# Seven block products instead of eight in the out-projection of the last four units of an RWKV + MLP kernel

## The chip, the cores and the metric

One core of one Trainium2 chip runs the kernel. The metric is the device time of one execution in microseconds (us), the median of several runs. TensorE (PE in the profile) multiplies matrices, VectorE (DVE), ScalarE (ACT) and GpSimd (POOL) work elementwise, SyncE (SP) issues most of the transfers. "PEld" is the loading of a matmul's stationary operand, which the profile shows as an instruction of its own.

## The reference

An RWKV-6 attention block feeds a two-layer MLP. Everything is float32.

```python
# attention: B, H, S, D = 4, 8, 768, 48
for t in range(S):
    cur = einsum('bhd,bhe->bhde', u[None] * k[:, :, t], v[:, :, t])
    y[:, :, t] = einsum('bhd,bhde->bhe', r[:, :, t], state + cur)
    state = w[:, :, t][:, :, :, None] * state + einsum('bhd,bhe->bhde', k[:, :, t], v[:, :, t])
x = y.transpose(0, 2, 1, 3).reshape(3072, 384)
# MLP: d_model = 384, d_ff = 2048
h = x @ w_in                       # (3072, 384) @ (384, 2048)
g = h * erf(softplus(h))
out = g @ w_out                    # (3072, 2048) @ (2048, 384)
```

## The kernel before

**Units and steps.** The 3072 tokens are cut into 12 units of 256 tokens: two batches (`NJ = 2`, index `j`) times 128 positions (`C`). Step `s` of the main loop does the attention of unit `s`. The MLP follows at a distance: `hidden(s - 1)` computes and activates the hidden values of the unit before, and `project(s - 3)` is the out-projection of the unit three back. In `in_order(s, k)` a letter string says how the pieces are laid between the parts of a step: `P` is one piece of `project`, `H` one piece of `hidden`, `A` one call of `advance`, which runs waiting activation stages (softplus or erf on ACT, or the DVE product `h * erf(...)`) from the list `later`. Steps up to 4 use `attend`, later ones `attend_late`. After step 11, the last, the loop `for k in range(1, 15)` runs what is left: the rest of `project(9)`, `hidden(11)`, `project(10)`, `project(11)`.

**Order.** The whole program stands in a manual schedule: each engine takes its instructions in the order in which the code issues them, and waits by semaphore for its operands and for buffers to come free. So an instruction that waits holds up what stands behind it on its own engine.

**The MLP's tiles.** `hidden` keeps the activated values of a unit in two tiles (`gs[0]`, `gs[1]`), one for each half of d_ff; each is 128 partitions (d_ff within a block) x 8 blocks (`FG`) x 256 tokens. `w_in_sb` and `w_out_sb` hold the weights for the whole kernel. `hidden` (L742) does three matmuls of 128x128 by 128x256 for each of the 16 blocks, and ACT copies each pair out of PSUM (L751). `project` (L771) does for each batch `j` 16 matmuls with a 128x128 stationary block of `gs` and 384 moving columns of `w_out_sb`, accumulates them in one PSUM tile (`ps_m`, two buffers, shared with `hidden`), copies that with ACT (L780) and sends it out on the SP queue (L781). Eight pieces (`P`) of four matmuls make one unit. Each float32 matmul stands in the profile as two pieces: 12 units x 32 matmuls are the "x768" of L771, 12 x 48 the "x1152" of L742.

**The activations.** For each of the two tiles ACT runs softplus (L724) and erf (L727), each behind a load of its function table, and DVE multiplies in two halves of 128x1024 (L731).

**Attention in the late steps.** `attend_late(s)` begins with PE products of the unit before (`from_own`, L478), a DVE `fence` (L487) that PE's next products wait for, level products (L444), and `through_state` (L504), which ends the unit before; its result goes by ACT and DMA into `xT`, which `hidden` reads. Alongside, `prepare(s + 1)` readies the next unit with POOL products (L312, L374, L378), DVE products and sums, and a last part: `scale` at the near level (L260), then the product of `block_sb` with `by_tokens` (L418), which comes back from DRAM.

**Buffers named below.** `rk1` (pool `att`) is scratch of the attention; `w` (pool `ins`) holds an input; `words` (pool `wide`, three buffers) holds inputs by rows and scratch. The last of them are read in the preparation of unit 11, which takes place in step 10.

Of the kernel before, what the change touches and what calls it, by code (L numbers as in the profile page):

```python
# [11 lines left out]
FP32 = mybir.dt.float32  # L12
I32 = mybir.dt.int32
# [2 lines left out]
ALU = mybir.AluOpType  # L16

P = 128
EP = 64
HC = 64  # L20
NC = 2
NJ = 2
FG = 8
# [37 lines left out]
def kernel(  # L61
# [14 lines left out]
    nc = tc.nc  # L76
    PSUM = bass.MemoryType.PSUM

    n_steps, _, _, JP, C = rkw.shape
# [4 lines left out]
    _, NT, DM = w_out.shape  # L84
    KT = DM // P
    UNIT = NJ * C
    NG = NT // FG
    SPC = NB // NJ
# [3 lines left out]
    const = ctx.enter_context(tc.tile_pool(name="const", bufs=1))  # L92
    ins = ctx.enter_context(tc.tile_pool(name="ins", bufs=2))
    att = ctx.enter_context(tc.tile_pool(name="att", bufs=2))
    xs = ctx.enter_context(tc.tile_pool(name="xs", bufs=3))
    hid = ctx.enter_context(tc.tile_pool(name="hid", bufs=4))
    act = ctx.enter_context(tc.tile_pool(name="act", bufs=2))
    wide = ctx.enter_context(tc.tile_pool(name="wide", bufs=4))
    outs = ctx.enter_context(tc.tile_pool(name="outs", bufs=2))
# [3 lines left out]
    ps_m = ctx.enter_context(tc.tile_pool(name="ps_m", bufs=2, space=PSUM))  # L103
# [17 lines left out]
    u_row = const.tile([P, D], FP32, name="u_row")  # L121
    w_in_sb = const.tile([P, NT, DM], FP32, name="w_in_sb")
    w_out_sb = const.tile([P, NT, DM], FP32, name="w_out_sb")
    y = ps_y.tile([P, NE, NJ, NP // 2, C], FP32, name="y")

    turns = {"next": 0, "converting": False}
# [40 lines left out]
    def near_log(s):  # L167
        return NEAR_LOG - (s == DIRECT)
# [85 lines left out]
    def scale(s, level):  # L254

        in_t, tots = loaded[s][0], ready[s][1]
        half, nb = 1 << (level - 1), JP * C >> level
        n = 1 if s > DIRECT and level == LOG else 2
        halves = view(in_t[:, 0:2], half, [[JP * C - half, n], [2 * half, nb], [1, half]])
        nc.vector.tensor_mul(  # L260
            halves, halves, view(tots[level - 1], 0, [[1, n], [2, nb], [0, half]])
        )

    def prepare(s):
# [3 lines left out]
        if s < DIRECT:  # L268
            rk1 = att.tile([P, 2, JP, C], FP32, name="rk1", bufs=1)
# [59 lines left out]
        else:  # L329
# [4 lines left out]
            to = over_blocks[:].rearrange("p (h b) n -> p b h n", h=NC)  # L334
# [76 lines left out]
        if near == NEAR:  # L411
# [2 lines left out]
                out=kTs[s][:], in_=k_blocks[:].rearrange("(g b) s d -> (b s) g d", g=NH)  # L414
            )
        scale(s, near_log(s))
        nb = HC // NEAR
        nc.vector.tensor_mul(  # L418
            own[:].rearrange("p n (b t) -> p n b t", t=NEAR),
# [2 lines left out]
            ),  # L422
            by_tokens[:, :, None, :].to_broadcast([P, NH, nb, NEAR]),
        )

    kTs, spread = {}, {}

# [136 lines left out]
    def attend_late(s, place):  # L564

        c, in_t, vt, own, S, S_next, ends = parts_of(s)
        RK = in_t[:, 0:2]
        before = s - 1 if s - 1 > DIRECT else None
        if before:
            from_own(before, ready[before][0], 1)  # L570
            fence()
        pp = products([P, NE, JP, HC])
        level_products(pp, RK, LOG - 1)
        scale(s, LOG - 1)
        take_level(own, pp, LOG - 1)
        if before:
            from_own(before, ready[before][0], 0)
            through_state(before, xTs[before])
            if s + 1 < n_steps:
                load_step(s + 1)  # L580
        following = prepare(s + 1) if s + 1 < n_steps else iter(())
        next(following, None)
        nc.gpsimd.tensor_mul(faded[0][:], S[:], ends[:, :, 0:1].to_broadcast([P, JP, D]))
        next(following, None)
        kT = kTs[s]
        nc.vector.tensor_mul(
            kT[:].rearrange("p (e n) d -> p n e d", e=NE),
            kT[:].rearrange("p (e n) d -> p n e d", e=NE), spread[s][:],
        )
        place(0)  # L590
        next(following, None)
        place(1)

        pp = products([P, NE, JP, HC])
        level_products(pp, RK, LOG)
        if s + 1 < n_steps:
            spread_blocks(s + 1, pp)
        take_level(own, pp, LOG)
        ps = products([P, NC, JP, HC])
        ps = [ps[:, h] for h in range(NC)]  # L600
        state_part(s, kT, ps)
        scale(s, LOG)
        for e in range(NE):
            nc.vector.tensor_add(middle[rows(e)], faded[0][rows(e)], ps[0][rows(e), :, :D])
        place(2)
        next(following, None)
        if s < n_steps - SPC:
            nc.gpsimd.tensor_mul(
                faded[1][:], middle[:], ends[:, :, 1:2].to_broadcast([P, JP, D])
            )  # L610
            for e in range(NE):
                nc.vector.tensor_add(S_next[rows(e)], faded[1][rows(e)], ps[1][rows(e), :, :D])
        place(3)
        for _ in following:
            pass
        place(4)
# [95 lines left out]

    later = []

    def hidden(xT, gs, cut):


        def activate(h):

            held = []  # L720

            def softplus():
                held.append(act.tile([P, FG, UNIT], FP32, name="sp"))
                nc.scalar.activation(held[0][:], h[:], AF.Softplus)  # L724

            def erf():
                nc.scalar.activation(held[0][:], held[0][:], AF.Erf)  # L727

            def multiply():
                for part in (slice(0, FG // 2), slice(FG // 2, FG)):  # L730
                    nc.vector.tensor_mul(h[:, part], h[:, part], held[0][:, part])  # L731

            later.extend([(softplus, True), (erf, True), (multiply, False)])

        for g in range(NG):
            h = hid.tile([P, FG, UNIT], FP32, name="h")
            gs.append(h)
            for f in range(0, FG, FT):
                ps = ps_m.tile([P, FT, UNIT], FP32, name="m")
                for ff in range(FT):  # L740
                    for kk in range(KT):
                        nc.tensor.matmul(  # L742
                            ps[:, ff, :],
                            lhsT=w_in_sb[:, g * FG + f + ff, kk * P : (kk + 1) * P],
                            rhs=xT[:, kk, :],
                            start=kk == 0,
                            stop=kk == KT - 1,
                        )
                    if cut and not ff and g == NG - 1 and f == FG - FT:
                        yield  # L750
                nc.scalar.copy(h[:, f : f + FT, :], ps[:])  # L751
                if f == FG - FT:
                    activate(h)
                yield

    def project(s, gs):

        c, i = divmod(s, SPC)
        ps = [None] * NJ

        halves = [slice(0, FG // 2), slice(FG // 2, FG)]
        for g in range(NG):
            for j, part in (
                [(j, part) for part in halves for j in range(NJ)]
                if not s and g == NG - 1
                else [(j, part) for j in range(NJ) for part in halves]
            ):
                if not g and not part.start:
                    ps[j] = ps_m.tile([P, DM], FP32, name="m")
                for f in range(FG)[part]:  # L770
                    nc.tensor.matmul(  # L771
                        ps[j][:],
                        lhsT=gs[g][:, f, j * C : (j + 1) * C],
                        rhs=w_out_sb[:, g * FG + f, :],
                        start=g + f == 0,
                        stop=g == NG - 1 and f == FG - 1,
                    )
                    if g == NG - 1 and f == FG - 1:
                        o = outs.tile([P, DM], FP32, name="o")
                        nc.scalar.copy(o[:], ps[j][:])  # L780
                        nc.sync.dma_start(out=out[i * NJ + j, c], in_=o[:])  # L781
                    if f % 4 == 3:
                        yield

    xTs, hids, projs = {}, {}, {}
    gated = [[] for _ in range(n_steps)]

# [18 lines left out]
    def piece(kind, of):  # L806
        if not 0 <= of < n_steps:
            return
        if of not in kind:
            kind[of] = hidden(xTs[of], gated[of], not of) if kind is hids else project(of, gated[of])  # L810
        next(kind[of])

    def in_order(s, k):


        order = ("APPPAPP", "APPP", "HH", "AHHH", "AHHH", "PPAPP")
        if s == DIRECT:
            order = ("APPP", "APPP", "APPHH", "AHHH", "AHHH")
        for what in order[k]:
            if what == "A":  # L820
                advance()
            elif what == "P":
                piece(projs, s - 3)
            else:
                piece(hids, s - 1)
# [13 lines left out]
    }  # L839
    ALONE = {1, 2}  # L840

    make_identity(nc, ident[:])
    nc.vector.memset(y[:], 0.0)
    nc.vector.memset(sums[:], 0.0)
# [176 lines left out]
```

## Time and profile before

| | |
|---|---|
| median of 3 runs | 616.99 us (616.94 to 617.49) |
| span of the profiled execution | 614.9 us |
| PE busy | 602.1 us (98%), 6858 matmul pieces |
| DVE busy | 409.3 us (67%) |
| ACT busy | 293.9 us (48%) |
| POOL busy | 293.3 us (48%) |
| L771 (out-projection) | 252.1 us busy, 768 pieces |
| L742 (hidden) | 257.3 us busy, 1152 pieces |

The span runs from the first to the last instruction or transfer that the profile shows; the device time that is compared between kernels holds in addition what lies around it. No separate device time is given for the profiled execution; the median of the runs is 2.1 us above the span. "Busy" is the union of the records of an engine. The mean duration of a record is its latency: matmuls overlap, so the time from one to the next is read from the busy time of a stretch divided by its pieces.

### The profile page before, as it was taken

The page shows a single profiled execution, that of the slowest core. Times are in us where ns is not written, and L with a number is a line of the kernel's source. Part 1 is how long each engine was busy: PE and PEld are TensorE (multiplying, and loading weights), DVE is VectorE, ACT ScalarE, POOL GpSimd, SP SyncE. Part 2 cuts the span into 40 slices and gives each one's busy share as a digit, 9 for nine tenths or more (in the row PEclk, how much of TensorE's full clock was granted, in tenths as well). Part 3 has the DMA queues.
Part 4 walks back from the last instruction along what each step waited for, and adds up shares of the span by engine and source line. Part 5 has one row for each costly group of instructions (what it writes and reads, how often), then busy time and mean ns, then how long its engine had stood idle before and what let it go on. Part 6 is the DMA issues. An engine that isn't in the chain of part 4 may idle for free.

```text
span 614.9 us, 15592 instructions
## 1 busy us (share of the span) xinstructions
PE 602.1 (98%) x6858; PEld 445.9 (73%) x6858; DVE 409.3 (67%) x459; ACT 293.9 (48%) x374; POOL 293.3 (48%) x295
## 2 busy tenths in 40 slices
PE   7889999999999999999999999999999999999997
PEld 6668787678668668668668768768768768668654
DVE  5687696995995897897797797797797311110300
ACT  2548888544446724534534534534534444624600
POOL 4348184603497399299199299299296000000000
PEclk9999999999999999999999999999999999999999
DMA  8376471440353316307307306405303100000000
GB/s 325 117 281 203 184 258 58 164 149 8 136 157 78 101 34 190 112 29 206 101 30 197 109 31 181 126 31 156 117 28 79 25 26 0 9 26 1 0 27 26
DMA packets 51371, 63.27 MB, mean 103 GB/s; under 512 B 34920, under 2 KB 40296, under 8 KB 49896
## 3 DMA queue, kind: packets, MB, share of 16 engines
q1 hardware_dynamic: 50152, 61.68, 31.5%
q8 instruction: 54, 0.88, 0.6%
q10 hardware_dynamic: 1152, 0.59, 0.4%
q14 instruction: 13, 0.11, 0.1%
HBM read 52.39 MB, written 8.69 MB: 99 GB/s over the span
## 4 chain that ended last, share of the span: by engine, by line
PE 85%; DVE 6%; DMA 3%; POOL 2%; issue 2%; ACT 1%; SPq 0%; POOLq 0%; ACTq 0%; DVEq 0%
PE m L771 38%; PE m L742 37%; PE pp L444 4%; DMA w<-in_rkw 3%; PE y L478 2%; PE y L504 1%; PE pp L530 1%; DVE in L260 1%; POOL w_in_sb L229 1%; DVE w_in_sb L225 1%; POOL tot_sb L312 1%; PE pp L673 1%; DVE sums L364 1%; DVE pp L217 1%; DVE own L456 1%
## 5 line engine op out<-in xcount | busy, mean ns | idle before, releaser
L742 PE MATMUL m<-xT,w_in_sb 128*128 128x256 f32 x1152 | 257.3, 382 | 2.4 <-DVE w_in_sb L225 1.2
L771 PE MATMUL m<-w_out_sb,h 128*128 128x384 f32 x768 | 252.1, 488 | 0.0
L742 PEld LDWEIGHTS m<-xT,w_in_sb 128*128 128x128 f32 x1152 | 216.1, 190 | 34.8 <-issue 3.6
L771 PEld LDWEIGHTS m<-w_out_sb,h 128*128 128x128 f32 x768 | 144.6, 190 | 98.5
L751 ACT COPY h<-m 128x512 f32<-128x512 f32 x96 | 56.1, 584 | 130.5 <-PE m L742 130.4
L731 DVE TENSOR_TENSOR h<-h,sp 128x1024 f32<-128x1024 f32 x48 | 74.6, 1594 | 52.1 <-ACT sp L727 51.9
L260 DVE TENSOR_TENSOR in<-in,tot_sb 128x1024 f32<-128x1024 f32 (+1 forms) x60 | 84.4, 1414 | 30.6 <-PE pp L444 27.3
L378 POOL TENSOR_TENSOR words<-words,rest 128x528 f32<-128x528 f32 (+10 forms) x77 | 85.7, 1113 | 6.0
L374 POOL TENSOR_TENSOR rk<-words 128x528 f32<-128x528 f32 (+3 forms) x28 | 44.5, 1588 | 81.2 <-DVE sums L364 70.8
L780 ACT COPY o<-m 128x384 f32<-128x384 f32 x24 | 11.5, 480 | 110.3 <-PE m L771 110.3
L312 POOL TENSOR_TENSOR tot_sb<-tot_sb 128x256 f32<-128x256 f32 (+4 forms) x60 | 54.6, 911 | 4.5
L727 ACT ACTIVATE sp<-sp 128x2048 f32<-128x2048 f32 x24 | 45.9, 1911 | 0.3
L724 ACT ACTIVATE sp<-h 128x2048 f32<-128x2048 f32 x24 | 45.9, 1911 | 0.3
L444 PEld LDWEIGHTS pp<-in 48*64 48x64 f32 (+1 forms) x2368 | 33.8, 125 | 16.3 <-issue 8.5
L364 DVE TENSOR_REDUCE sums<-words 128x6 f32<-128x288 f32 (+8 forms) x66 | 29.2, 470 | 19.4 <-POOL words L374 19.2
L444 PE MATMUL pp<-in 48*64 48x64 f32 (+1 forms) x2368 | 38.3, 212 | 3.7 <-issue 1.6
L727 ACT ACT_TABLE_LOAD x24 | 30.8, 1283 | 15.9 <-issue 13.0
L374 POOL TENSOR_TENSOR words<-words 128x336 f32<-128x336 f32 (+6 forms) x49 | 35.1, 716 | 3.8
L364 DVE TENSOR_REDUCE sums<-rk 128x14 f32<-128x672 f32 (+9 forms) x54 | 34.8, 704 | 0.2
L724 ACT ACT_TABLE_LOAD x24 | 30.8, 1283 | 4.9 <-issue 4.5
L378 DVE TENSOR_TENSOR words<-words,rest 128x576 f32<-128x576 f32 (+8 forms) x34 | 27.9, 820 | 1.2
L229 POOL TENSOR_TENSOR w_out_sb<-w_out_sb,rest 128x768 int32<-128x768 int32 x8 | 17.8, 2222 | 17.8 <-DVE w_out_sb L225 17.7
(80 smaller groups left out, 438.0 us busy)
## 6 DMA issues: line engine op xcount, KB each, us to landing
in<-in_rkw SPq DMA_DIRECT2D x11, 1024.0 KB, 5.6
words<-in_moe_w_in SPq DMA_DIRECT2D x8, 768.0 KB, 4.5
words<-in_moe_w_out SPq DMA_DIRECT2D x8, 768.0 KB, 4.3
words<-in_rk_rows SPq DMA_DIRECT2D x8, 768.0 KB, 6.8
w<-in_rkw SPq DMA_DIRECT2D x11, 512.0 KB, 8.4
v<-in_v SPq DMA_DIRECT2D x12, 384.0 KB, 6.9
out<-o SPq DMA_DIRECT2D x24, 192.0 KB, 1.9
rest<-in_w_rows SPq DMA_DIRECT2D x8, 384.0 KB, 7.3
```

What stands on the lines that cost most here:

```text
L260: nc.vector.tensor_mul(halves, halves, view(tots[level - 1], 0, [[1, n], [2, nb], [0, half]]))
L312: nc.gpsimd.tensor_mul(new, pair[:, :, 0], pair[:, :, 1])
L364: nc.vector.tensor_reduce(out=view(sums[:], n, [[near * (NEAR + 1), NEAR // near], [NEAR + 1, near - n]]), in_=terms[n], axis=mybir.AxisLi ...
L374: engine.tensor_mul(terms[n], r[:, :, n:], k[:, :, : near - n])
L378: engine.tensor_mul(k[:, :, :m], k[:, :, :m], w[:, :, n : n + m])
L444: nc.tensor.matmul(pp[s0 : s0 + m, e, n, :m], lhsT=rk[rows(e), 1, n, s0 : s0 + m], rhs=rk[rows(e), 0, n, t0 : t0 + m], start=True, stop=True,)
L724: nc.scalar.activation(held[0][:], h[:], AF.Softplus)
L727: nc.scalar.activation(held[0][:], held[0][:], AF.Erf)
L731: nc.vector.tensor_mul(h[:, part], h[:, part], held[0][:, part])
L742: nc.tensor.matmul(ps[:, ff, :], lhsT=w_in_sb[:, g * FG + f + ff, kk * P : (kk + 1) * P], rhs=xT[:, kk, :], start=kk == 0, stop=kk == KT - 1,)
L751: nc.scalar.copy(h[:, f : f + FT, :], ps[:])
L771: nc.tensor.matmul(ps[j][:], lhsT=gs[g][:, f, j * C : (j + 1) * C], rhs=w_out_sb[:, g * FG + f, :], start=g + f == 0, stop=g == NG - 1 and ...
```

## The change

The products of the last four units (`FAST = 8`: units 8 to 11) take another form. For a unit, the activations are a 2 x 2 block matrix (batch `j` by half of d_ff) and so are the weights (half of d_ff by half of the 384 output columns, 192 each). Instead of the eight block products of the plain form, `project_fast` does seven (the Strassen-Winograd form), each of eight matmuls 128x128 by 128x192. It needs:

- sums of the weights, made by `mix_weights` in four DVE operations of 128x1536 elements: three go into the new tile `mixed`, the fourth replaces a quarter of `w_out_sb` in place. They are issued in the last part of `prepare(9)`, `prepare(10)` and `prepare(11)`, that is, in steps 8, 9 and 10; in step 10 there are two.
- sums of the activations, made by `blend` in four DVE operations of 128x1024 for each unit. For unit 8 they are issued in step 11, ahead of the `kT` product; for units 9 to 11 they follow the last activation product of the unit in `later`.
- recombination: ACT copies of PSUM after the first, third and fourth product, and a DVE addition after the sixth and after the seventh, behind each of which an output row block is sent out.

The seven products are seven pieces; from step 11 on the letter strings have seven `P` for a unit instead of eight. The pool `xs` (the tiles `xT`) has two buffers instead of three, and the DMA scratch is set to 1024; the sums of activations use `rk1`, `w` and `words`.

```diff
+FAST = 8
-    xs = ctx.enter_context(tc.tile_pool(name="xs", bufs=3))
+    xs = ctx.enter_context(tc.tile_pool(name="xs", bufs=2))
+    ND = DM // NJ
+    mixed = const.tile([P, 3, FG, ND], FP32, name="mixed")
...
         scale(s, near_log(s))
+        if s > FAST:
+            next(mixing)
         nb = HC // NEAR
         nc.vector.tensor_mul(
             own[:].rearrange("p n (b t) -> p n b t", t=NEAR),
...
+        if s == FAST + 3:
+            next(mixing)
...
         next(following, None)
+        if s == FAST + 3:
+            blend(FAST, gated[FAST])
         kT = kTs[s]
...
             later.extend([(softplus, True), (erf, True), (multiply, False)])
+            if of > FAST and len(gs) == NG:
+                later.append((lambda: blend(of, gs), False))
...
+    def mix_weights():
+        upper, lower = w_out_sb[:, :FG], w_out_sb[:, FG:]
+        b11, b12, b21, b22 = (x[:, :, k * ND : (k + 1) * ND] for x in (upper, lower) for k in range(2))
+        t3, t2, t4 = (mixed[:, n] for n in range(3))
+        nc.vector.tensor_sub(t3, b22, b12)
+        yield
+        nc.vector.tensor_add(t2, t3, b11)
+        yield
+        nc.vector.tensor_sub(t4, b21, t2)
+        yield
+        nc.vector.tensor_sub(b12, b12, b11)
+        yield
...
+    def blend(of, gs):
...
+        nc.vector.tensor_add(s1, a21, a22)
+        nc.vector.tensor_sub(s2, s1, a11)
+        nc.vector.tensor_sub(s4, a12, s2)
+        nc.vector.tensor_sub(a21, a11, a21)
+        blends[of] = s1, s2, a21, s4
...
+    def project_fast(s, gs):
...
+        product(m0[:, lo], a11, b11, True)
+        nc.scalar.copy(o[0][:, lo], m0[:, lo])
+        yield
+        product(m1[:, lo], a22, t4, True)
+        yield
+        product(m1[:, hi], s1, t1, False)
+        nc.scalar.copy(o[1][:], m1[:])
+        yield
+        product(m0[:, lo], s2, t2, False)
+        nc.scalar.copy(o[0][:, hi], m0[:, lo])
+        yield
+        product(m1[:, hi], s4, b22, False)
+        yield
+        product(m0[:, lo], s3, t3, False)
+        halves = o[1][:].rearrange("p (k n) -> p k n", k=2)
+        nc.vector.tensor_add(halves, halves, m0[:, None, lo].to_broadcast([P, 2, ND]))
+        nc.sync.dma_start(out=out[i * NJ + 1, c], in_=o[1][:])
+        yield
+        product(m1[:, lo], a12, b21, True)
+        nc.vector.tensor_add(o[0][:], o[0][:], m1[:])
+        nc.sync.dma_start(out=out[i * NJ, c], in_=o[0][:])
+        yield
...
-            kind[of] = hidden(xTs[of], gated[of], not of) if kind is hids else project(of, gated[of])
+            if kind is hids:
+                kind[of] = hidden(of, xTs[of], gated[of], not of)
+            else:
+                kind[of] = (project_fast if of >= FAST else project)(of, gated[of])
...
         order = ("APPPAPP", "APPP", "HH", "AHHH", "AHHH", "PPAPP")
+        if s >= FAST + 3:
+            order = ("PAPPPAP", "PAP", "HH", "AHHH", "AHHH", "PPPAP")
...
+    mixing = mix_weights()
-    nc = bacc.Bacc("TRN2", target_bir_lowering=False, num_devices=1)
+    nc = bacc.Bacc("TRN2", target_bir_lowering=False, num_devices=1, dynamic_dma_scratch_size=1024)
```

## The prediction

> **What bounds the kernel now.** I read the page first: busy shares, slices, chain. Then the chain in order of time, for the last fifth of the run.
>
> ```profile
> span 614.9 us, 15592 instructions
> PE 602.1 (98%) x6858; PEld 445.9 (73%) x6858; DVE 409.3 (67%) x459; ACT 293.9 (48%) x374; POOL 293.3 (48%) x295
> ...
> PE   7889999999999999999999999999999999999997
> PEld 6668787678668668668668768768768768668654
> DVE  5687696995995897897797797797797311110300
> ...
> PEclk9999999999999999999999999999999999999999
> ```
>
> PE is busy all the time from the fourth slice on, at the full granted clock. DVE has gaps of two to three tenths in steps 5 to 10 and is nearly idle from slice 32 on (step 11 and the tail).
>
> ```profile
> 531.24 18.26 PE m L771 x56
> 549.49 20.72 PE m L742 x96
> 570.21 41.29 PE m L771 x128
> 611.57 0.48 ACT o L780
> ```
>
> The chain at the end is nothing but MLP matmuls one behind another. So PE time taken out of units 8 to 11 comes off the end one for one, as long as nothing new makes PE wait. Two questions remain: what a piece with 192 columns costs, and whether DVE delivers its sums in time.
>
> **The price of a piece.** I take it from stretches where PE does only one kind: 64 pieces of 384 columns in 20.84 us (436.81 to 457.65) are 0.3256 us each, and 96 pieces of 256 columns in 20.92 us (366.45 to 387.37, in the chain) are 0.2179 us. The line through both has 0.000841 us a column and about 2.5 ns fixed, so 192 columns cost 0.2179 - 64 x 0.000841 = 0.164 us. Before, four units took 256 x 0.3256 = 83.4 us. Now they take 4 units x 7 products x 8 matmuls x 2 pieces = 448 pieces x 0.164 = 73.5 us. **The sum for PE: 9.9 us less**, 2.46 us a unit.
>
> That holds only if the loads of the stationary operand, 448 instead of 256, stay hidden:
>
> ```profile
> 436.81:457.65 20.84, 20.84 (x64) 12.01 (x64) 1.00 0.24 85
> ```
> ```profile
> L771 PEld LDWEIGHTS m<-w_out_sb,h 128*128 128x128 f32 x768 | 144.6, 190 | 98.5
> ```
> ```profile
> L852 PEld LDWEIGHTS m<-ident 128*128 128x128 f32 x19 | 2.2, 192 | 0.0
> ```
> ```profile
> 183.80 0.86 PEld L673 LDWEIGHTS pp<-ident,in 128*128 128x128 f32 x8
> 183.80 1.09 PE L673 MATMUL pp<-ident,in 128*128 128x128 f32 x8
> ```
>
> The first line is the projection of one unit (columns: stretch, length, PE busy, loads busy): 64 loads fill 12.01 us, 0.188 us each, so nowhere in L771 do two loads overlap each other. A record of 0.190 us is longer than the 0.164 us that I want to give a piece; if 0.190 were the rate, there would be no gain. The third line decides: in the warm-up from 6 to 8 us, 19 loads of 0.192 us stand in 2.2 us, so they overlap and come every 0.116 us or faster, each with a 128-column matmul behind it. The transposes of L673, with a different stationary block each time, load 8 in 0.86 us, 0.108 us each. 0.190 is a latency, and 0.116 is under 0.164.
>
> [...] the L771 pieces follow each other at 0.3256 us, what 384 columns cost at the slope alone (0.323), so there is no room for a load in series. I use the row.
>
> For the 192-column piece the ends are 0.160 us (slope alone: 71.7 us, 11.7 us less) and 0.190 us (85.1 us, 1.8 us more); I take 0.164, because the slope joins measured rows and the warm-up shows loads faster than that. Some products wait for two engines, for which PE may need a separate semaphore instruction; the five in L771 last 0.051 us. If all 28 products paid one, that would be 1.4 us; I take 0, since the L771 stretches show no such gap, and keep it in the range.
>
> **DVE: sums of weights.** No row has 128x1536. With POOL idle, 128x768 takes 0.947 us (L586 in step 11) and 128x1024 takes 1.222 us (L731 after 480 us), so 1536 cost about 1.77 us. At the place where they go in steps 8 and 9, the scale just ahead takes 1.42 us instead of 1.21 with POOL running, so 2.07 us there; with the worst factor on the page's shape (2.1 against 1.21) 3.1. The cover is DVE's wait:
>
> ```profile
> 384.67 1.23 DVE L418 TENSOR_TENSOR own<-block_sb,by_tokens 128x1024 f32<-128x1024 f32 x1 [0.34 <-DMA by_tokens<-by_blocks]
> 388.03 0.17 DVE L487 COPY seen<-y 128x16 f32<-128x16 f32 x1 [2.13 <-PE y L478]
> ...
> 434.31 0.17 DVE L487 COPY seen<-y 128x16 f32<-128x16 f32 x1 [2.46 <-PE y L478]
> ...
> 476.79 1.23 DVE L418 TENSOR_TENSOR own<-block_sb,by_tokens 128x1024 f32<-128x1024 f32 x1 [2.02 <-DMA by_tokens<-by_blocks]
> 480.87 0.17 DVE L487 COPY seen<-y 128x16 f32<-128x16 f32 x1 [2.86 <-PE y L478]
> ```
>
> The fence L487 is what PE's second group of L478 waits for, and behind the new operation only L418 and the fence stand in its way. Step 8: 0.34 + 2.13 = 2.47 us idle against 2.07. Step 9: 2.46 against 2.07. Step 10: 2.02 + 2.86 = 4.88 against 2 x 1.77 = 3.54; the in-place one waits for project(7), which PE has done in the first half of the step. PE itself needs the fence only about 0.5 us later (388.66). Cost taken: 0; at 3.1 us each, about 0.1 us in each of two steps.
>
> **DVE: unit 8 in step 11.** Four sums at 1.22 us start where kT started, 483.56, and end at 488.5. PE begins product 1 at 483.08 and one product lasts 16 x 0.164 = 2.63 us. Product 3 (s1) begins at 488.3 and s1 is there at 484.8; product 4 at 491.0 needs s2 (486.0) and the ACT copy of product 1, which stands behind ACT's DMA issues until 486.94 and is done at 487.4. The kT product ends at 489.5; the activation product behind it started at 490.18 before anyway. Cost 0.
>
> **DVE and ACT: units 9 and 10.** Their blends run after 506 and 545 in a DVE that was idle for 18 and 31 us there; they are needed more than 12 us later. Cost 0.
>
> **Unit 11** is the tight one. Project(10) now begins at 570.21 - 2 x 2.46 = 565.3 and ends at 583.7. ACT has copies of 0.3 to 0.5 us and three activation stages of 1.28 + 1.91 = 3.19 us between them: copy 1 at 568.3, erf 571.5, copy 576.1, softplus 579.3, erf 582.5. DVE is worse: the addition behind product 7 waits for PE until 583.7 and ends at 584.3 (0.55 us, as L604), and behind it on DVE stand the last activation product (2 x 1.22, to 586.7), then s1 (587.9), s2 (589.2), s4, s3 (591.6). PE: product 1 of unit 11 needs only the first tile, 583.7 to 586.3; product 2 needs the second tile's first half at 586.3 (there at 585.5) and its second at 587.6 (586.7); product 3 needs s1 at 588.9, 1.0 us after it is there; the others have over 2 us. Cost 0, with a reserve of 0.8 to 1.0 us.
>
> **Rest.** The last ACT copy (0.48) becomes a DVE addition (about 0.55): +0.07 us. The output transfers are as many and as large; the two of a unit change order, and SP has nothing else to do there but xT's. With two `xT` buffers, a write waits for hidden() of two units back, which PE ended a step earlier: 0. The DMA scratch: every queue on the page is "hardware_dynamic" or "instruction" and none is named for such a scratch, so 0.
>
> **Sum.** 614.9 - 9.86 + 0.07 = 605.1 us span. The median of the runs lies 2.1 us above the span of the profiled execution, which I keep: **607.2 us**.
>
> **Rivals.** (a) DVE late at unit 11 or at a fence. If sums and activation products took 1.77 us there, as L260 does beside POOL, s1 would come at 589.6, 0.6 us late; with the fences (0.2) and the semaphore instructions (1.4) about 2 us: 609.4. POOL is idle after slice 32, which speaks against it. (b) Load-bound pieces, the slower side: PE cannot overlap loads when each has a fresh operand[...]. At 0.190 us a piece the change costs 85.1 - 83.4 = +1.8 us: 618.8. It decides from 83.4 / 448 = 0.186 us on. The L771 loads that never overlap speak for it, L852 and L673 against. (c) Half of that: loads at about 0.175 us, 78.4 us, 612. (d) The change does not do what it says: the sevenths are not saved because products repeat; the instruction order has 56 matmuls of 192 columns a unit in place of 32 of 384, so no.
>
> **Chances.** Forecast as worked out 0.80 (606 to 608.4), (a) 0.11, (b) 0.05, (c) 0.03, anything else 0.01. The range 606.0 to 609.7 takes in the forecast and (a). About 0.2%, 1.2 us, is what a measurement of this kernel can tell from no change: faster 0.93, same 0.02, slower 0.05.
>
> **What would show it.** Right: the new product line has 448 pieces in about 73.5 us; a unit's seven products take 18.4 us; loads of that line overlap each other; PE waits for DVE nowhere at its third product; hidden(11) begins at about 544.6 and the last product ends at 601.7. Wrong: 0.19 us a piece with PEld full (b); a PE wait on a `blend` result, or fence waits gone in steps 8 and 9 with PE idle before L478's second group (a).

## The result, and the profile after

The changed kernel takes 608.01 us (median of 4 runs, 607.56 to 609.0) against 617.24 us for the kernel before (the three executions of the table above and a fourth): 0.9851 of its time, 95% interval 0.9837 to 0.9865. A second series gave 607.39 us against 617.23 us: 0.9837 (0.9823 to 0.9850). The forecast was 607.2 us, with a range of 606.0 to 609.7. Some executions of these kernels have a mean granted clock of 0.992 to 0.997 and are 1 to 4 us longer than the others of the same kernel; all eight of the changed kernel here have 0.999 or 1.00.

The page of the changed kernel: its head and some of its slices:

```profile
span 605.9 us, 16024 instructions
...
PE 592.9 (98%) x7050; PEld 470.8 (78%) x7050; DVE 439.5 (73%) x487; ACT 294.3 (49%) x378; POOL 296.1 (49%) x295
...
PE   8889999999999999999999999999999999999997
...
PEclk9999999999999999999999999999999999999999
```

PE is as full as before and at the same clock, over a span that is 9.0 us shorter, with 192 matmul pieces more. DVE has 30 us more work (409.3 to 439.5). The line numbers move: `project` is L782 now, and the new products are L844, `hidden` is L753, the fence is L494.

The end of the chain of waits, in order of time (start, length, what):

```profile
483.72 18.40 PE m L844 x112
...
525.17 2.80 PE m L844 x16
...
529.46 15.80 PE m L844 x96
545.25 20.72 PE m L753 x96
565.97 36.41 PE m L844 x224
602.47 0.56 DVE o L868
```

The reader sees the same chain as before: MLP matmuls one behind another, with no link to DVE between them. Units 10 and 11 take 36.41 us where they took 41.29.

### The profile page after: what moved, and what is told of

It reads as the page before. It is cut to its first block, busy times and chain, and to the rows that moved or that the text cites. A ratio compares the mean times of both kernels' runs of the same rounds, so it can differ in the third digit from the quotient of the medians.

```text
span 605.9 us, 16024 instructions
## 1 busy us (share of the span) xinstructions
PE 592.9 (98%) x7050; PEld 470.8 (78%) x7050; DVE 439.5 (73%) x487; ACT 294.3 (49%) x378; POOL 296.1 (49%) x295
## 4 chain that ended last, share of the span: by engine, by line
PE 85%; DVE 7%; issue 2%; POOL 2%; ACT 2%; DMA 1%; SPq 0%; DVEq 0%; POOLq 0%; ACTq 0%
PE m L753 38%; PE m L782 25%; PE m L844 12%; PE pp L451 5%; DVE in L263 2%; PE y L485 2%; PE y L511 1%; PE pp L537 1%; POOL w_in_sb L232 1%; DMA in<-in_rkw 1%; DVE w_in_sb L228 1%; PE pp L682 1%; DVE sums L367 1%; DVE pp L220 1%; DVE own L463 1%
## 5 line engine op out<-in xcount | busy, mean ns | idle before, releaser
L753 PE MATMUL m<-xT,w_in_sb 128*128 128x256 f32 x1152 | 257.3, 382 | 2.4 <-DVE w_in_sb L228 1.2
L753 PEld LDWEIGHTS m<-xT,w_in_sb 128*128 128x128 f32 x1152 | 216.1, 190 | 34.6 <-issue 3.6
L782 PE MATMUL m<-w_out_sb,h 128*128 128x384 f32 x512 | 168.6, 489 | 0.0
L782 PEld LDWEIGHTS m<-w_out_sb,h 128*128 128x128 f32 x512 | 96.2, 190 | 65.3
L315 POOL TENSOR_TENSOR tot_sb<-tot_sb 128x256 f32<-128x256 f32 (+4 forms) x60 | 57.6, 960 | 4.5
L451 PEld LDWEIGHTS pp<-in 48*64 48x64 f32 (+1 forms) x2368 | 33.8, 125 | 16.1 <-issue 8.3
L451 PE MATMUL pp<-in 48*64 48x64 f32 (+1 forms) x2368 | 38.4, 212 | 3.8 <-issue 1.6
L791 ACT COPY o<-m 128x384 f32<-128x384 f32 x16 | 7.7, 478 | 65.6 <-PE m L782 65.6
```

The source lines that it names most:

```text
L315: nc.gpsimd.tensor_mul(new, pair[:, :, 0], pair[:, :, 1])
L451: nc.tensor.matmul(pp[s0 : s0 + m, e, n, :m], lhsT=rk[rows(e), 1, n, s0 : s0 + m], rhs=rk[rows(e), 0, n, t0 : t0 + m], start=True, stop=True,)
L753: nc.tensor.matmul(ps[:, ff, :], lhsT=w_in_sb[:, g * FG + f + ff, kk * P : (kk + 1) * P], rhs=xT[:, kk, :], start=kk == 0, stop=kk == KT - 1,)
L782: nc.tensor.matmul(ps[j][:], lhsT=gs[g][:, f, j * C : (j + 1) * C], rhs=w_out_sb[:, g * FG + f, :], start=g + f == 0, stop=g == NG - 1 and ...
```

## The experiments

**1. What a load costs: fewer columns.** Everything rests on the price of a piece. Cutting the same products into narrower pieces makes the loads more and the columns of each fewer, until the load shows.

```diff
+        parts = {8: 2, 9: 3, 10: 4, 11: 1}[s]
         def product(to, a, b, start):
-            for f in range(FG):
-                nc.tensor.matmul(to, lhsT=a[:, f], rhs=b[:, f], ...
+            n = ND // parts
+            for q in range(parts):
+                part = slice(q * n, (q + 1) * n)
+                for f in range(FG):
+                    nc.tensor.matmul(to[:, part], lhsT=a[:, f], rhs=b[:, f, part], ...
```

> The seven products of units 8, 9 and 10 are cut into columns: two pieces of 96, three of 64, four of 48 in place of one of 192, each with all its stationary blocks loaded again; unit 11 stays at 192. The arithmetic is the same. Theory (a piece costs its columns as long as that is more than the time of a load): the changed kernel has 0.1625 us for 192 columns; if loads never bind, 96, 64 and 48 columns cost 0.082, 0.056 and 0.042 us and the three units stay at 18.4 to 19 us each, under 2 us in all. If a load of 128 columns takes about 0.107 us and hides behind the matmul before it, all three kinds cost about 0.107 us: the units take 24.0, 36.0 and 47.9 us, some 53 us more than the changed kernel. Rival (a load holds the engine 0.190 us, or cannot overlap with a matmul): 0.19 us a piece, 42.6, 63.8 and 85.1 us, over 135 us more.

It took 707.8 us. PE's timeline shows two later products of each kind, and then two of unit 11 at 192 columns (start, length, instructions):

```profile
486.94 3.74 PE L849 MATMUL m<-mixed,h 128*128 128x96 f32 x32
490.51 3.74 PE L849 MATMUL m<-w_out_sb,rk 128*128 128x96 f32 x32
...
543.92 5.52 PE L849 MATMUL m<-w_out_sb,words 128*128 128x64 f32 x48
549.28 5.52 PE L849 MATMUL m<-mixed,words 128*128 128x64 f32 x48
...
613.00 13.85 PE L849 MATMUL m<-w_out_sb,rk 128*128 128x48 f32 x64
626.65 13.85 PE L849 MATMUL m<-mixed,rk 128*128 128x48 f32 x64
...
689.09 2.76 PE L849 MATMUL m<-w_out_sb,words 128*128 128x192 f32 x16
691.69 2.76 PE L849 MATMUL m<-mixed,words 128*128 128x192 f32 x16
```

The record of one piece is longer than the time to the next (0.326 us at 192 columns in the changed kernel), so the price is read from start to start: (490.51 - 486.94) / 32 = 0.1116 us at 96 columns, (549.28 - 543.92) / 48 = 0.1117 us at 64, 2.60 / 16 = 0.1625 us at 192. Two widths with one price: the columns no longer set it. It is not the mere issue of instructions either: the 64 short attention products of L451, each with its own smaller load, take 0.93 us in the chain of the changed kernel, 0.0145 us each. What is left is the load: 241 loads stand in the 26.80 us of the later 64-column products, and PE is busy all that time. So a load of 128x128 comes every 0.112 us (the expectation took 0.107; the eight loads of L673 in 0.86 us, which the prediction shows, are 0.108 us each), hidden behind running matmuls, and by an estimate it binds below about 131 columns (0.112 us on the line through 0.1625 us at 192 and 41.29 / 128 = 0.3226 us at 384). The change at 192 columns lies on the safe side, by a factor of 1.45 in time. Rival (b), 0.190 us a piece, falls.

Units 8 and 9 took 25.2 and 37.7 us, where 24.0 and 36.0 were expected. Unit 10 took 89.8 us instead of 47.9: the 48-column pieces shown cost 13.65 / 64 = 0.213 us, twice as much, which neither theory expected. The next run is about that.

**2. The clock at 48 columns.** The edit is the same with `{8: 4, 9: 1, 10: 3, 11: 4}`.

> As the run cut into columns, with another assignment: unit 8 and unit 11 in pieces of 48 columns, unit 10 in pieces of 64, unit 9 at 192. There the 48-column unit ran at half the granted clock from its first product on, and the 64-column unit at the full one. [...]units 8 and 11 both drop to 0.213 us a piece (95 us a unit) and unit 10 stays at 0.112; if it was the length of the MLP stretch without attention, or its place at the end of the run, unit 8 keeps the full clock at 0.112 us a piece (50 us).

774.58 us. First unit 8's first product, then a table by stretch for the later products of unit 8 (48 columns), unit 10 (64) and unit 11 (48); the columns of the table are the stretch, its length, PE busy, loads busy, granted clock, DMA:

```profile
483.18 8.72 PE L849 MATMUL m<-w_out_sb,h 128*128 128x48 f32 x64
```

```profile
491.71:573.62 81.91, 81.91 (x385) 81.91 (x385) 0.50 0.01 3
646.11:672.91 26.80, 26.80 (x243) 26.80 (x242) 1.00 0.00 1
687.19:755.45 68.26, 68.26 (x321) 68.26 (x322) 0.50 0.00 1
```

Wherever the 48 columns stand, PE counts as busy all the time, and yet the granted clock is 0.50 in these stretches. It does not start so, as the expectation had it: unit 8's first product takes only 8.53 us from start to start. The clock is 1.00 for its first 5.7 us, in which pieces of 48 columns follow each other every 0.112 us like those of 64 and 96, and then falls to 0.50; unit 11 here and unit 10 of run 1 show the same after 5.2 and 6.2 us. So the load has one price at three widths, and the step to 0.213 us comes with the clock: at 0.50 the loads too come every 0.213 us (385 in 81.91 us). At 64 columns the clock stays at 1.00 for 27 us. So position and the absence of attention are ruled out. The fall goes with the width, 48 columns against 64; what in the width brings it about is not shown.

**3. The sums alone.** The sums are made at their places, into scratch, and the out-projection stays plain.

```diff
-        nc.vector.tensor_sub(b12, b12, b11)
+        nc.vector.tensor_sub(t3, b12, b11)
-        nc.vector.tensor_sub(a21, a11, a21)
+        nc.vector.tensor_sub(s1, a11, a21)
-                kind[of] = (project_fast if of >= FAST else project)(of, gated[of])
+                kind[of] = project(of, gated[of])
-        if s >= FAST + 3:
-            order = ("PAPPPAP", "PAP", "HH", "AHHH", "AHHH", "PPPAP")
```

> All sums of weights and activations are made at the same places as in the changed kernel, but into scratch, and the out-projection stays in its plain form with 384 columns for all units; the sums are read by nobody. Theory (DVE's waits cover the sums): no difference to the kernel before beyond 0.3 us, 616.9 to 617.5; fence waits of about 0.8 us left in steps 8 and 9. Rival (sums or the new layout of buffers cost PE time): 0.6 us or more above the kernel before, with idle PE at the fence of steps 8 to 10 or at the start of the kernel.

617.59 us against 617.29: 1.0009 (1.0000 to 1.0018), 0.1 us above the expected range and at the edge of what can be told from nothing. Single executions go from 616.6 to 619.9 us here and from 616.6 to 619.1 in the kernel before. Without those at a mean granted clock of 0.994 to 0.997, five of 20 here and three of 23 there, the medians are 617.45 and 617.26 us. The first trace has a span of 616.3 us and still shows fence waits of 0.77 and 0.73 us in steps 8 and 9. A second trace was taken of the same kernel:

> The kernel with all sums made and the plain out-projection kept, once more for its trace; its timed runs went from 616.6 to 619.9 us. Theory: the sums cost PE nothing, and what differs from the kernel before lies in PE's stalls without a releaser (1.55 us in step 6 in its first trace, 0.94 us in the kernel before). Rival: PE waits for the fence or for sums.

617.49 us. In this trace step 8's out-projection begins at 344.32 us, in the first at 344.90, in the kernel before at 343.96; from there to the beginning of the last stretch of matmuls (570.73, 571.31 and 570.21) all three need 226.3 to 226.4 us, and that stretch takes 41.29 us in each. The sums cost PE at most 0.2 us; the rest of the difference between these traces lies ahead of step 8, where no sum is made yet.

**4. The products alone.**

```diff
-        if s > FAST:
-            next(mixing)
-        if s == FAST + 3:
-            next(mixing)
-        if s == FAST + 3:
-            blend(FAST, gated[FAST])
-            if of > FAST and len(gs) == NG:
-                later.append((lambda: blend(of, gs), False))
-        s1, s2, s3, s4 = blends[s]
+        a21 = gs[0][:, :, C:]
+        s1, s2, s3, s4 = a21, a12, a21, a22
-        t3, t2, t4 = (mixed[:, n] for n in range(3))
+        t3, t2, t4 = b22, b21, t1
```

> The seven products without any sums: the sums of weights and of activations are left out and each product takes a plain block of the activations and of the weights, so the output is not the reference's; copies, additions and transfers stay. Theory (the sums are fully covered): the same as the changed kernel within 0.5 us, 607.4 to 608.5, seven products in 18.2 to 18.4 us. Rival (products of units 8 to 11 wait for sums): 1 us or more faster than the changed kernel, below 607.

607.54 us, 0.984 of the kernel before (0.9823 to 0.9856). From the first product of unit 8 to the beginning of the last addition its chain has 483.45 to 602.19, 118.74 us; the changed kernel has 483.72 to 602.47, 118.75 us. With all sums taken away, PE gains nothing there: they are fully covered.

**5. The reserve at unit 11.**

```diff
-        nc.vector.tensor_add(s1, a21, a22)
+        for _ in range(3 if of == 11 else 1):
+            nc.vector.tensor_add(s1, a21, a22)
```

> The first activation sum of unit 11 alone is issued three times instead of once (the same result). In the changed kernel it ended at 588.34 us and the third product of unit 11, which reads it, began at 589.21: a reserve of 0.87 us. Theory: two more at 1.26 us put its end at 590.86, product 3 begins 1.65 us late, and everything behind it follows: 1.65 us slower than the changed kernel, about 609.7. Rival (the wait is absorbed, because weight loads and later products can go ahead, or because the end is set by the outputs): under 0.3 us slower.

609.5 us (0.9887, 0.9844 to 0.9931), 1.5 us above the first series of the changed kernel and 2.1 above the second. Its four executions go from 608.55 to 613.58 us, the last at a mean granted clock of 0.992. The trace shows the wait where it was forecast. First DVE and PE of the changed kernel, then PE of this one:

```profile
584.26 0.55 DVE L868 TENSOR_TENSOR o<-o,m 128x384 f32<-128x384 f32 x1 [2.04 <-PE m L844]
584.74 2.35 DVE L740 TENSOR_TENSOR h<-h,sp 128x1024 f32<-128x1024 f32 x2
587.12 1.22 DVE L823 TENSOR_TENSOR words<-h 128x1024 f32<-128x1024 f32 x1
```

```profile
589.21 2.76 PE L844 MATMUL m<-w_out_sb,words 128*128 128x192 f32 x16
```

```profile
591.13 2.87 PE L845 MATMUL m<-w_out_sb,words 128*128 128x192 f32 x16 [1.55 <-DVE words L824]
```

In the changed kernel s1 is there at 588.34 and product 3 begins at 589.21, 0.87 us later. Two repeats of 1.26 us eat that and leave 1.65; PE waits 1.55 us for `words`, and all that follows moves with it. So the addition behind product 7, for which DVE waits while the last activation product stands behind it, is the place with the smallest reserve of the change.

**6. The reserve at the fence.** The weight sums of steps 8 and 9 twice:

```diff
-        nc.vector.tensor_sub(t3, b22, b12)
+        for _ in range(2):
+            nc.vector.tensor_sub(t3, b22, b12)
-        nc.vector.tensor_add(t2, t3, b11)
+        for _ in range(2):
+            nc.vector.tensor_add(t2, t3, b11)
```

> The weight sums of steps 8 and 9 are each issued twice (the same result): 1.84 us more on DVE ahead of the fence in each of the two steps. In the changed kernel the fence still waited 0.76 us for PE there, and PE's next group of products reads the fence's mark about 0.5 us after it. Theory (that wait is all the cover there is): the fence comes 1.08 us later in both steps and PE stands still for 0.5 to 0.6 us in each, some 1.1 us slower than the changed kernel. Rival (DVE's lateness passes on to the next step, where other waits take it up, and PE does not see it): under 0.3 us slower. Second rival (it adds up through the chain of DVE, GpSimd and fence): 2 us or more.

610.7 us in the median of 608.61, 610.1, 611.29 and 611.78; the trace is of the first. Two more traces were taken of the same kernel:

> The kernel with the weight sums of steps 8 and 9 issued twice, once more for its trace: its timed runs spread from 608.6 to 611.8 us while the traced one was 608.6, with 0.6 and 0.4 us more in front of PE's second group in steps 8 and 9. If the spread comes from the chain of DVE, GpSimd and fence, a slower execution shows longer fence waits of PE in steps 8 to 10 (over 1.5 us in all); if it comes from PE's stalls without a releaser, those in steps 6 and 10 are longer (over 2 us in all) and the fence waits are as before.

> The same a third time: a slower execution shows either longer fence waits of PE in steps 8 to 10, or longer PE stalls without a releaser in steps 6 and 10.

608.75 and 609.07 us. All three traces agree on the wait. Step 8 in the changed kernel, DVE and PE, then in the first trace of this run, DVE and PE:

```profile
384.65 1.84 DVE L801 TENSOR_TENSOR mixed<-w_out_sb 128x1536 f32<-128x1536 f32 x1
...
388.43 0.17 DVE L494 COPY seen<-y 128x16 f32<-128x16 f32 x1 [0.76 <-PE y L485]
```

```profile
387.70 0.66 PE L485 MATMUL y<-own,v 64*48 64x64 f32 x32
389.12 0.63 PE L485 MATMUL y<-own,v 64*48 64x64 f32 x32
```

```profile
388.65 1.23 DVE L423 TENSOR_TENSOR own<-block_sb,by_tokens 128x1024 f32<-128x1024 f32 x1
389.92 0.17 DVE L494 COPY seen<-y 128x16 f32<-128x16 f32 x1
```

```profile
388.14 0.67 PE L485 MATMUL y<-own,v 64*48 64x64 f32 x32
390.15 0.66 PE L485 MATMUL y<-own,v 64*48 64x64 f32 x32 [0.41 <-DVE seen L494]
```

From the first to the second group of L485 it is 2.01 us here (388.14 to 390.15) and 1.42 us in the changed kernel (387.70 to 389.12): 0.59 us more, and 0.38 us more in step 9. In step 8 the other two traces have 2.03 and 1.99 us. The sum, 1.0 us, is the difference of the spans (606.8 against 605.8 us in the second series' trace). The theory holds for what the traces show.

The median is another matter: it lies 3.3 us above the changed kernel, which is the second rival's figure, but that rival's chain is in no trace. The three executions above 610 us have mean granted clocks of 0.997, 0.997 and 0.992, the first has 1.00. The third trace, at 0.997, shows what such a mean can be: one spell of about 3.4 us at half the clock, between 15 and 22 us, after which step 5's out-projection begins at 205.19 instead of 204.33 us. Neither its fence waits nor its stop in step 6 (1.02 us, 1.36 in the first trace) is longer. No trace holds an execution above 610 us, so when their clock falls, and how much of their time that takes, stays open.

**7. A fifth unit.** If PE alone sets the end, unit 7 should give another 2.4 us. Its sums do not fit into DVE's step 10, so GpSimd makes them, in the hole in its work:

```diff
-        if s > FAST:
+        if FAST - 1 <= s <= FAST + 2:
             next(mixing)
...
+        if s == FAST + 2:
+            blend_early(FAST - 1)
...
+    def blend_early(of):
...
+        nc.gpsimd.tensor_add(s1, a21, a22)
+        nc.gpsimd.tensor_sub(a21, a11, a21)
+        blends[of] = s1
+        piece(projs, of)
+        piece(projs, of)
+        nc.gpsimd.tensor_sub(s1, s1, a11)
+        nc.gpsimd.tensor_sub(a11, a12, s1)
```

> A fifth unit, unit 7, gets the seven products, in step 10. Its two rooms fit nowhere else, so its sums are made by GpSimd in the hole between its work for the two preparations (434 to 447 us in the kernel before), in one free input buffer and in place in the activations, between the first two products; the weight sums move one step ahead, one in each of steps 6 to 9. Theory (PE sets the end and the sums are covered): 2.4 us faster than the changed kernel, about 605.5. Rival (GpSimd and DVE slow each other down in the hole, and the late sums reach PE): no gain or slower, with PE idle before the fourth or fifth product of unit 7 or before the fence of step 11.

621.5 us: 1.0065 of the kernel before (1.0051 to 1.0079), some 14 us above the changed kernel. The rival won. GpSimd, DVE and PE of step 10, and in between two lines of DVE in the changed kernel:

```profile
441.24 3.07 POOL L883 TENSOR_TENSOR w<-w,h 128x1024 f32<-128x1024 f32 x1
444.38 2.91 POOL L884 TENSOR_TENSOR h<-h,w 128x1024 f32<-128x1024 f32 x1
```

```profile
442.01 3.05 DVE L377 TENSOR_TENSOR rk<-words 128x720 f32<-128x720 f32 x1
445.10 2.95 DVE L381 TENSOR_TENSOR words<-words,rest 128x720 f32<-128x720 f32 x1
448.09 0.86 DVE L377 TENSOR_TENSOR rk<-words 128x672 f32<-128x672 f32 x1
...
469.54 0.54 DVE L921 TENSOR_TENSOR o<-o,m 128x384 f32<-128x384 f32 x1
```

```profile
438.26 0.90 DVE L377 TENSOR_TENSOR rk<-words 128x720 f32<-128x720 f32 x1
...
440.14 0.86 DVE L377 TENSOR_TENSOR rk<-words 128x672 f32<-128x672 f32 x1
```

```profile
470.13 23.61 PE L753 MATMUL m<-xT,w_in_sb 128*128 128x256 f32 x96 [9.57 <-DVE o L921]
```

A DVE product of 0.90 us takes 3.05 us while GpSimd works, and the next one, of 0.86 us, takes 0.86 again as soon as GpSimd stops. The two run in lockstep: each of the two long DVE products ends about 0.75 us after the GpSimd operation that began before it (445.06 after 444.31, 448.05 after 447.29). What holds the two together is not shown.

DVE is then about 8 us late (448.09 against 440.14 for the same instruction). The recombining addition stands behind it in DVE's queue and comes at 469.5; `hidden` needs its PSUM buffer, and PE stands still for 9.6 us. The clock falls in that idle time: it is 0.50 from 466 to 475 us (0.988 in the mean of this execution, 1.00 in that of the changed kernel), and the 96 pieces that follow take 23.61 us instead of 20.99. The lockstep is not all of it. By an estimate from these rows, without the 8 us the addition would come at about 461.6 us, while `hidden` begins at 459.93 in the changed kernel. By this estimate the addition's place in DVE's queue alone would have eaten the gain of 2.4 us.

**8. The changed kernel again.**

> The changed kernel as it is, beside the others on one chip. Theory: 607.5 to 608.5 us; the stretch from the first product of unit 8 to the end of the last addition 119.3 us as in its first trace, and what differs between its runs lies in PE's stalls without a releaser in steps 6 and 10.

607.39 us, 0.1 us below the expected range; step 11's products begin at 483.70 and end as in the first trace (565.97 and 36.41 us there, 565.95 and 36.41 here).

None of these edits makes the kernel faster than that.

## Why the prediction was right

- **The price of a piece** was put at 0.164 us. Inside a run of products it is 0.1625; the first product behind the short attention matmuls takes 2.71 us instead of 2.60 from start to start (483.65 to 486.36). The four units took 18.40 + 2.80 + 15.80 + 36.41 = 73.4 us, forecast 73.5; the stretches of the kernel before add up to 20.84 + 2.78 + 18.26 + 41.29 = 83.2 us, forecast 83.4. The gain is 9.76 us where the sum had 9.86. The 0.1 us comes from how the forecast divided: stretches that follow other MLP matmuls cost 41.29 / 128 = 0.3226 and 20.72 / 96 = 0.2158 us a piece, so its 0.3256 and 0.2179 hold about 0.2 us a stretch for the beginning.
- **Hidden loads.** The forecast read the overlap of loads from the warm-up and the transposes, 0.116 and 0.108 us; runs 1 and 2 measured 0.112. In the last stretch of L844, 223 loads of 0.190 us each stand in 36.27 us, one every 0.163: they overlap one another, as no load of L771 did (64 in 12.01 us, 0.188 each).
- **The weight sums** took 1.84 us in steps 8 and 9 (forecast 2.07) and 1.75 in step 10 (1.77), and left 0.76 us of the fence's wait. Run 6 shows that this wait and the half microsecond behind it are about all the cover there is.
- **Unit 11** came as worked out: s1 at 588.34 (587.9), product 3 at 589.21 (588.9), reserve 0.87 us (1.0). Run 5 shows that nothing else covers it.
- **The end**: the last addition takes 0.56 us where the copy took 0.48; forecast +0.07.
- **What the sum missed**: the span is 605.9 us and not 605.1. All but the 0.1 us above lies ahead of the changed products: those of step 11 begin 0.64 us later than in the kernel before. The median again lies 2.1 us above the span, as the forecast took it. PE's timeline of step 6 before, and of steps 6 and 10 after:

```profile
250.92 0.44 PE L504 MATMUL y<-in,middle 48*48 48x64 f32 x16 [0.94 <-issue]
```

```profile
251.32 0.44 PE L511 MATMUL y<-in,middle 48*48 48x64 f32 x16 [1.26 <-issue]
...
436.57 0.37 PE L511 MATMUL y<-in,s 48*48 48x64 f32 x10 [0.22 <-issue]
```

Both kernels stop in step 6 in the middle of a group of equal matmuls, waiting for nothing that the profile shows; the changed kernel stops once more in step 10, where the kernel before does not. The stop in step 6 was 1.02 to 1.55 us in the other traces of kernels with the changed layout of buffers, 1.16 in the one without any sums. So sums are not its cause; whether the new layout makes it longer, or the one trace of the kernel before was a short one, stays open. It is 0.1% of the time.

Rival (a) did not come, but runs 5 and 6 made its mechanism happen at both places, at close to the expected prices: 1.55 us where 1.65 was expected, and 0.59 and 0.38 us where 0.5 to 0.6 was. Rivals (b) and (c) are ruled out by the price of 0.1625 us in the changed kernel and by run 1; (d) by the 224 pieces for units 10 and 11 in the chain, seven eighths of the columns of 128 pieces of 384.

## What to carry to other kernels

Trading one matmul in eight for elementwise sums paid here, where TensorE set the end and the narrower pieces (0.1625 us) still lasted longer than a weight load (0.112 us). In another kernel, measure that load by cutting the columns until the price stops falling, not from the length of its record, which was a latency here (0.190 us), and read the granted clock beside it (0.50 at 48 columns). Then look for the waits that hide the sums, and know their size: here 0.87 us at unit 11, and at the fence 0.76 us of DVE's wait with about half a microsecond behind it. What went beyond that PE lost (1.55 us in run 5, 0.59 and 0.38 us in run 6). The idle stretch of GpSimd was no free room, for its operations held up those of DVE (3.05 us for 0.90 in run 7).

## What the runs showed of the hardware that was not expected

- The granted clock fell to 0.50 while PE counted as busy without a gap, 5.2 to 6.2 us after 48-column pieces began (0.112 us each before, 0.213 us after), and stayed at 1.00 with 64-column ones (0.112 us). The 48-column pieces of runs 1 and 2 lost half the clock besides the load's time.
- Loads of a 128x128 block follow each other every 0.112 us behind running matmuls, though the record of one lasts 0.190 us.
- DVE and GpSimd operations ran in lockstep: 0.90 us became 3.05 us for DVE beside GpSimd operations of 2.9 to 3.1 us.
